# A fused attention, expert and feed-forward kernel: second unit's scores in other PSUM banks, zero products ahead of the first scores, clears moved, the last tile in halves

## The chip, the cores and the metric

The kernel runs on one core of one Trainium2 chip, as a single launch. The metric is the device time of that launch in microseconds (us). Three runs of the kernel before took 1148.23, 1147.63 and 1146.03 us; their median, 1147.63 us, is the time before.

## The reference

The reference chains three parts over 2304 tokens (4 batches of 576) of width 512. Part one is attention with 8 heads of 64: scores are scaled by 1/8, scores more than `tau` below their row's maximum are masked out, and a softmax over what is left weights the values. Part two is a mixture of 8 experts, two for each token, chosen by noisy gate logits. Part three is a feed-forward layer with a leaky rectifier whose slope is given for each hidden unit.

```python
scores = scale * np.matmul(q, k.transpose(0, 1, 3, 2))
thresh = np.max(scores, axis=-1, keepdims=True) - tau
scores = np.where(scores >= thresh, scores, -1000000000.0)
attn = np.exp(scores - np.max(scores, axis=-1, keepdims=True))
attn = attn / (np.sum(attn, axis=-1, keepdims=True) + 1e-09)
x = np.matmul(attn, v)                       # then [tokens, 512]
# experts: for each token the two largest of x@w_gate + log1p(exp(x@w_noise))*noise
out[mask] += top2_w[mask, k, None] * (np.maximum(x[mask] @ w1[e], 0.0) @ w2[e])
# feed-forward
h = x @ w_in
g = np.maximum(h, 0.0) + alpha * np.minimum(h, 0.0)
return g @ w_out
```

All inputs but `w_in` and `w_out` are 32-bit floats. The kernel splits each operand of a large product into a high and a low part (rounded to the matmul's fast 32-bit type, and the rest), and adds three products: high by high, high by low, low by high.

## The kernel before, in words

**Attention.** Work is cut into units: a unit is one batch, one pair of heads and 128 rows of queries (or the 64 rows left over, the "t" units, with both heads in one block-diagonal tile). The first 16 units are batch 0, head pair by head pair: units 0 to 3 use the operands of pair 0, units 4 to 7 those of pair 1, and so on. A unit passes these steps, each a small function:

- `s_mm` (line 386): 12 products of 288 columns on TensorE give the scores of two heads, into two tiles of two PSUM banks each (`psum_s`, two buffers, so one unit holds all four banks of this pool).
- `d1` (L401): VectorE scales the scores out of PSUM and takes the row's extreme; one instruction for each head.
- `a1` (L412): ScalarE's exponential. `thresh` (L406) makes the mask's limit.
- `d2` (L425): VectorE masks and sums, one instruction for each head.
- `t_mm` (L443, L445): nine turns of 128 by 128 on TensorE; `a2` (L455, L457) copies them out.
- `pv` (L479, L481): products with the values; then ScalarE copies the result (L497).

The loop over `i` (L818) issues, in this order, `t_mm` and `a2` of unit `i - 2`, `d1` and `a1` of unit `i`, `d2` of unit `i - 1`, `s_mm` of unit `i + 1`, and `pv` of unit `i - 3`. The order of issue is the order on every engine. `put(i, f)` files a piece of other work to be issued at iteration `i`. Among it are `split_hi` (L328, L330: ScalarE rounds a raw operand) and `do_lo` (L338: GpSimd subtracts to get the low part; ahead of it a one-element copy, L734, makes GpSimd wait for the newest row sum of `d2`). After the low part of a query operand, `tail_tile` (L322) copies 64 by 64 blocks for the "t" units. The off-diagonal blocks of those tiles are cleared once: 32 memsets at L314, ahead of everything else on GpSimd. GpSimd then clears two tiles for the values (L347), makes the last part of the first low operand (L705), runs `tail_tile(0)`, and clears a tile of zeros (L708) that iterations 9 to 23 write to DRAM.

**The first unit.** Its operands are loaded in four pieces, rounded on ScalarE (L704), and their low parts made by VectorE (three pieces, L705) and GpSimd (the fourth).

**PSUM.** Four banks belong to `psum_s`; the other four to `psum_t` (three) and `psum_v` (one), which `t_mm` and `pv` first use at iterations 2 and 3.

**Experts and feed-forward.** After attention TensorE runs the expert layers (L236, L254) and the feed-forward (L236, L1103) nearly without a break. The last step, `down_chunk` (L1087) for the last chunk, finishes four output tiles in the order 0, 2, 1, 3: 12 products of 512 columns, three for each tile, each tile followed by a copy out of PSUM (ScalarE for 0 and 2, VectorE for 1 and 3, L1096) and a store (L1098) that SyncE issues.

Of the kernel before, what the change touches and what calls it, by code (L numbers as in the profile page):

```python
# [6 lines left out]
FT = mybir.dt.float32  # L7
# [18 lines left out]
NSET = 8  # L26
SETW = 2688
DT = 2
# [7 lines left out]
def emit(tc, qt, kt, v, tau, wg, wn, noise, w1, w2, w_in, w_out, alpha, out):  # L36
# [8 lines left out]
    with (  # L45
# [57 lines left out]
        pairs = tc.tile_pool(name="psum_pairs", bufs=1, space=PSUM)  # L103
        bank_pool = [pairs.__enter__()]

        def psum_s():
            return bank_pool[0].tile([128, 2, 512], FT, name="ps_s", tag="s", bufs=2)

        def single_banks():
            pairs.__exit__(None, None, None)  # L110
            bank_pool[0] = later.enter_context(tc.tile_pool(name="psum_banks", bufs=1, space=PSUM))
# [3 lines left out]

        def psum_t(dt=FT):
            return pp.tile([128, 512], dt, name="ps_t", tag="t", bufs=3)

        def psum_v():
            return pp.tile([128, 512], FT, name="ps_v", tag="v", bufs=1)  # L120
# [190 lines left out]
        for i in range(NSET):  # L311
            for z in pair(i)[4:]:
                for h in range(2):
                    pool.memset(f32(z[h * 64:h * 64 + 64, 64 - h * 64:128 - h * 64]), 0.0)  # L314
# [76 lines left out]
        def s_bank(i):  # L391
            for h in range(nh(i)):
                st[i]["ps", h] = psum_s()
# [312 lines left out]
        tail_tile(0)  # L706
        zero = xtok_ring()
        pool.memset(zero, 0.0)  # L708
# [44 lines left out]

        for e in range(E):
            put(9 + 2 * e, zero_init, e)
# [60 lines left out]
        s_bank(0)  # L816
        s_mm(0)
        for i in range(END):  # L818
            it, iv = i - DT, i - DT - 1
            tiles, outs = 0 <= it < NU, 0 <= iv < NU  # L820
            if tiles:
                t_mm(it, 0)
                a2(it, 0)
# [263 lines left out]
        def down_chunk(j, f):  # L1087
# [6 lines left out]
            def store(t):  # L1094
                y = y_tile[0]()
                (dve.tensor_copy if last and t % 2 else act.copy)(y, acc[j][t])  # L1096
                r = (sum(sizes[:j]) + t) * 128
                sp.dma_start(out[r:r + 128], y)  # L1098

            for t in (0, 2, 1, 3) if last else range(sizes[j]):  # L1100
                ps = acc[j][t]
                for k, (x, ww) in enumerate(((0, WH), (1, WH), (0, WL))):
                    pe.matmul(ps, h[x][:, t * 128:t * 128 + 128], ww[w][:, c:c + 512],  # L1103
                              start=(f == 0 and k == 0), stop=(f == 15 and k == 2))
                if last:
                    store(t)
# [151 lines left out]
```

## Time and profile before

| | us |
|---|---|
| median of three runs | 1147.63 |
| the profiled execution, its own time | 1147.74 |
| its span, first instruction to last | 1145.9 |
| TensorE busy | 1124.0 |
| VectorE busy | 612.6 |
| ScalarE busy | 528.5 |
| GpSimd busy | 534.1 |

The profiled execution took 1147.74 us; its span is 1145.9 us, so 1.8 us lie around it. A timeline row reads: start in us from the span's start, length in us, engine, line, operation, output and inputs, sizes and count; in brackets the idle time of the engine before it and what ended that. SPq is SyncE's queue, which issues DMAs; PEld is the loading of weights. A row with a count covers several instructions that follow each other, gaps included.

### The profile page before, as it was taken

Reading aid. Unit: us, or ns where it says so; the run is one execution under the profiler, and the core shown is the slowest. Engines: PE = TensorE matmul, PEld = TensorE weight load, DVE = VectorE, ACT = ScalarE, POOL = GpSimd, SP = SyncE. Lnnn points to the kernel's source line nnn. Section 1 sums busy time; section 2 is a strip of 40 time slices with the busy share of each in tenths; the row PEclk is TensorE's granted clock in tenths of the full one; section 3 lists DMA queues with packets and bytes.
Section 4 is the critical chain, followed back from the end, with each engine's and each line's share of the span. In section 5 each row is a group of like instructions: output and inputs, shape, how many; then the busy total and the mean of one; then the engine's idle time right before and its main releaser. Section 6 shows DMA issues by size and latency. Waiting matters only on the chain.

```text
span 1145.9 us, 20653 instructions
## 1 busy us (share of the span) xinstructions
PE 1124.0 (98%) x7754; PEld 974.0 (85%) x7754; DVE 612.6 (53%) x1316; ACT 528.5 (46%) x1039; POOL 534.1 (47%) x706
## 2 busy tenths in 40 slices
PE   7999999999999999999999999999999999999997
PEld 6887888788898989888999999898888888888886
DVE  6879899699544544444444544444433443442221
ACT  7978888689344444445444545442111211121111
POOL 7556545554635455455554454484322332332221
PEclk9999999999999999999999999999999999999999
DMA  6423222232566766667767565532321321220001
GB/s 212 142 94 120 101 97 85 88 118 83 187 175 190 192 205 183 189 179 220 192 172 222 175 187 188 179 121 65 74 56 55 74 54 53 73 56 23 21 1 39
DMA packets 156553, 141.51 MB, mean 123 GB/s; under 512 B 108576, under 2 KB 109216, under 8 KB 156448
## 3 DMA queue, kind: packets, MB, share of 16 engines
q1 hardware_dynamic: 150400, 120.91, 36.1%
q0 software_dynamic: 5760, 18.88, 5.0%
q8 instruction: 63, 1.03, 0.4%
q14 instruction: 42, 0.34, 0.1%
q10 hardware_dynamic: 288, 0.34, 0.1%
HBM read 97.11 MB, written 42.99 MB: 122 GB/s over the span
## 4 chain that ended last, share of the span: by engine, by line
PE 69%; issue 3%; POOL 2%; DVE 2%; ACT 1%; DMA 1%; SPq 0%; POOLq 0%; DVEq 0%; ACTq 0%
PE ps_t L236 33%; PE ps_u L1103 17%; PE ps_u L254 16%; POOL m_pair L190 1%; PE ps_v L479 0%; DMA m_tmp<-in_w_in_dram 0%; PE ps_u L236 0%; ACT m_hh L412 0%; DMA m_v<-in_w_dram 0%; PE ps_t L216 0%; POOL m_tmp L956 0%; DVE m_tmp L401 0%; PE ps_t L443 0%; ACT m_last L455 0%; POOL m_last L190 0%
## 5 line engine op out<-in xcount | busy, mean ns | idle before, releaser
L236 PE MATMUL ps_t<-m_v,m_pair 128*128 128x384 f32 (+2 forms) x1216 | 220.1, 317 | 0.6 <-ACT m_v L220 0.3
L190 POOL TENSOR_TENSOR m_pair<-m_v,m_pair 128x512 fp32r<-128x512 f32 x108 | 143.7, 1352 | 121.8 <-ACT m_pair L184 111.3
L236 PEld LDWEIGHTS ps_t<-m_v,m_pair 128*128 128x128 f32 x1216 | 186.8, 190 | 8.8 <-ACT m_v L220 0.7
L254 PE MATMUL ps_u<-m_pair,m_hh 128*128 128x512 f32 x528 | 167.5, 390 | 0.0
L1080 DVE TENSOR_SCALAR m_tmp<-ps_t,alpha_t 128x512 f32<-128x512 f32 (+1 forms) x80 | 55.7, 697 | 208.6 <-PE ps_t L236 206.7
L247 DVE SCALAR_TENSOR_TENSOR m_gate<-ps_t,m_hh 128x384 fp32r<-128x384 f32 (+1 forms) x120 | 58.9, 493 | 169.2 <-ACT m_hh L246 169.0
L236 PE MATMUL ps_t<-m_v,m_early 128*128 128x256 f32 (+2 forms) x672 | 127.3, 320 | 0.0
L401 DVE TENSOR_SCALAR_CACHE_REDUCE m_tmp<-ps_s 128x576 f32<-128x576 f32 x144 | 106.1, 753 | 29.4 <-ACT m_last L457 12.7
L425 DVE SCALAR_TENSOR_TENSOR m_hh<-m_tmp,sm,m_hh 128x576 f32<-128x576 f32 x144 | 117.3, 847 | 0.0
L254 PEld LDWEIGHTS ps_u<-m_pair,m_hh 128*128 128x128 f32 x528 | 99.2, 188 | 20.2
L1085 POOL TENSOR_TENSOR m_v<-m_tmp,m_v 128x512 fp32r<-128x512 f32 x39 | 50.5, 1294 | 140.0 <-ACT m_v L1084 140.0
L236 PEld LDWEIGHTS ps_t<-m_v,m_early 128*128 128x128 f32 x672 | 105.8, 189 | 5.1 <-DVE m_v L224 0.4
L412 ACT ACTIVATE m_hh<-m_tmp,sm 128x576 f32<-128x576 f32 x144 | 105.5, 782 | 3.2 <-DVE m_tmp L401 3.2
L1084 ACT CAST m_v<-m_tmp 128x512 fp32r<-128x512 f32 x39 | 24.2, 621 | 173.7 <-DVE m_tmp L1081 173.7
L254 PE MATMUL ps_u<-m_pair,m_gate 128*128 128x512 f32 x264 | 103.0, 390 | 0.0
L1085 POOL TENSOR_TENSOR m_gate<-m_tmp,m_gate 128x512 fp32r<-128x512 f32 (+1 forms) x41 | 44.1, 1078 | 115.8 <-ACT m_gate L1084 109.6
L246 ACT ACTIVATE m_hh<-ps_t 128x384 fp32r<-128x384 f32 (+1 forms) x120 | 52.7, 439 | 98.5 <-PE ps_t L236 97.0
L386 PE MATMUL ps_s<-m_pair 64*128 64x288 f32 (+1 forms) x864 | 89.1, 317 | 9.0 <-ACT m_pair L704 4.4
L1103 PE MATMUL ps_u<-m_pair,m_v 128*128 128x512 f32 x396 | 95.1, 389 | 0.0
L1103 PE MATMUL ps_u<-m_pair,m_gate 128*128 128x512 f32 x360 | 88.3, 391 | 0.0
L386 PEld LDWEIGHTS ps_s<-m_pair 64*128 64x128 f32 (+1 forms) x864 | 69.4, 191 | 22.3 <-DVE m_tmp L401 11.9
L1103 PEld LDWEIGHTS ps_u<-m_pair,m_v 128*128 128x128 f32 x396 | 74.3, 188 | 15.4
(244 smaller groups left out, 1987.8 us busy)
## 6 DMA issues: line engine op xcount, KB each, us to landing
m_v<-in_w_dram SPq DMA_DIRECT2D x64, 512.0 KB, 4.0
yg<-m_tmp SPq DMA_DIRECT2D x40, 256.0 KB, 3.3
m_tmp<-in_w_in_dram SPq DMA_DIRECT2D x16, 512.0 KB, 4.3
m_tmp<-in_w_out_dram SPq DMA_DIRECT2D x16, 512.0 KB, 5.1
m_early<-in_kt_dram SPq DMA_DIRECT2D x15, 320.0 KB, 3.5
yg<-m_gate SPq DMA_DIRECT2D x18, 256.0 KB, 2.0
m_rows<-xg SPq DMA_DIRECT2D x72, 64.0 KB, 3.1
out_dram<-m_tmp SPq DMA_DIRECT2D x18, 256.0 KB, 2.4
```

The source lines that it names most:

```text
L190: eng.tensor_tensor(WL[n][:, w], raw[:, w], f32(WH[n][:, w]), op=OP.subtract)
L236: pe.matmul(ps[:, :n], w[wc[d]][:, col:col + 128], x[xx][:, d, :n], start=(k == 0), stop=(k == 11))
L246: act.activation(h, ps, AF.Relu)
L247: dve.scalar_tensor_tensor(hs[1][:, f * n:f * n + n], ps, 0.0, f32(h), op0=OP.max, op1=OP.subtract)
L254: pe.matmul(ps, a[:, o:o + 128], ww[w][:, c:c + 512], start=(f == 0 and k == 0), stop=(f == nf - 1 and k == 2))
L386: pe.matmul(u["ps", h][:, x, :288], lhs, kk[r, o:o + 288], start=(k == 0), stop=(k == 2))
L401: dve.tensor_scalar(u["sp"][:, h].rearrange("p (a b) -> p a b", a=2), ps[:, :, :288], -0.125, None, op0=OP.mult, op1=OP.min, accum_out=u[" ...
L412: act.activation(u["em"][:, h], u["sp"][:, h], AF.Exp, bias=u["sm"][:, h:h + 1], scale=-1.0)
L425: dve.scalar_tensor_tensor(u["em"][:, h], u["sp"][:, h], sm[:, 2 + h:3 + h], u["em"][:, h], op0=OP.is_le, op1=OP.mult, accum_out=acc)
L1080: dve.tensor_scalar(g, ps, 0.0, alpha_t[:, f:f + 1], op0=OP.min, op1=OP.mult)
L1085: pool.tensor_tensor(h[:, n:2 * n], g, f32(h[:, :n]), op=OP.subtract)
L1103: pe.matmul(ps, h[x][:, t * 128:t * 128 + 128], ww[w][:, c:c + 512], start=(f == 0 and k == 0), stop=(f == 15 and k == 2))
```

## The change

Four edits, all at the head or the tail of the program.

1. The scores of unit 1 go into a pool of their own, `psum_first`, in the four banks that `psum_t` and `psum_v` use later; `second_half` closes it at iteration 2 (`i == DT`) and opens `psum_second` for those two. The two pools of scores move to the other side of PSUM.
2. A tile `spare` is zeroed by VectorE, and seven products of it with itself are issued on TensorE ahead of `s_mm(0)`, into columns of the first unit's bank that the scores don't use. At iteration 2 eight turns of the identity are issued ahead of `t_mm(0)`.
3. The 32 memsets at L314 become `clear_tails`, four of them at each of the iterations 1 to 8; `tail_tile(0)` moves to iteration 5, and the memset of the tile of zeros to iteration 7.
4. In the last step, output tile 3 is computed and stored in two halves of 256 columns, the first copied by ScalarE and the second by VectorE.

```diff
-        pairs = tc.tile_pool(name="psum_pairs", bufs=1, space=PSUM)
+        pairs = tc.tile_pool(name="psum_pairs", bufs=1, space=PSUM, side="right")
...
+        half = [tc.tile_pool(name="psum_first", bufs=1, space=PSUM)]
+        half.append(half[0].__enter__())
+
+        def second_half():
+            half[0].__exit__(None, None, None)
+            half[1] = later.enter_context(tc.tile_pool(name="psum_second", bufs=1, space=PSUM))
+
         def psum_t(dt=FT):
-            return pp.tile([128, 512], dt, name="ps_t", tag="t", bufs=3)
+            return half[1].tile([128, 512], dt, name="ps_t", tag="t", bufs=3)
...
-        for i in range(NSET):
+        def clear_tails(i):
             for z in pair(i)[4:]:
                 for h in range(2):
                     pool.memset(f32(z[h * 64:h * 64 + 64, 64 - h * 64:128 - h * 64]), 0.0)
...
-                st[i]["ps", h] = psum_s()
+                st[i]["ps", h] = half[1].tile([128, 2, 512], FT, name=f"ps_f{h}") if i == 1 else psum_s()
...
-        tail_tile(0)
         zero = xtok_ring()
-        pool.memset(zero, 0.0)
...
+        for n in range(NSET):
+            put(1 + n, clear_tails, n)
+        put(5, tail_tile, 0)
+        put(7, pool.memset, zero, 0.0)
...
         s_bank(0)
+        spare = em_ring.aps[2][:, 0, :128]
+        dve.memset(spare, 0.0)
+        for _ in range(7):
+            pe.matmul(st[0]["ps", 0][:, 0, 384:], spare, spare, start=True, stop=True)
         s_mm(0)
...
+            if i == DT:
+                second_half()
+                ps = psum_v()
+                for _ in range(8):
+                    pe.transpose(ps[:, :128], ident, ident)
...
-            def store(t):
-                y = y_tile[0]()
-                (dve.tensor_copy if last and t % 2 else act.copy)(y, acc[j][t])
+            def store(t, o=0, n=512):
+                y = y_tile[0]()[:, o:o + n]
+                (dve.tensor_copy if last and (t == 1 or o) else act.copy)(y, acc[j][t][:, o:o + n])
                 r = (sum(sizes[:j]) + t) * 128
-                sp.dma_start(out[r:r + 128], y)
+                sp.dma_start(out[r:r + 128, o:o + n], y)
...
+                for o, n in ((0, 256), (256, 256)) if last and t == 3 else ((0, 512),):
+                    for k, (x, ww) in enumerate(((0, WH), (1, WH), (0, WL))):
+                        pe.matmul(ps[:, o:o + n], h[x][:, t * 128:t * 128 + 128], ww[w][:, c + o:c + o + n],
```

On TensorE the program begins, before, with the scores of units 0 to 2 (three times 12 products at L386), then the turns of unit 0 (L443, L445) and the scores of unit 3:

```order
L1254 UNCONDITIONAL_BRANCH
L386 MATMUL ps_s<-m_pair 128x288 x36
L443 MATMUL ps_t<-ident,m_hh 128x128 x8
L445 MATMUL ps_s<-ident,m_hh 128x128
L386 MATMUL ps_s<-m_pair 128x288 x12
L443 MATMUL ps_t<-ident,m_hh 128x128 x8
L445 MATMUL ps_s<-ident,m_hh 128x128
L386 MATMUL ps_s<-m_pair 128x288 x12
L479 MATMUL ps_v<-m_tmp,m_v_73 64x128 x8
L481 MATMUL ps_v<-m_tmp,m_v_73 64x128 x2
```

Each row there is a run of equal instructions; the lines from 386 to 705 stand 7 higher in the changed program. Now, with what each waits for (DVE is VectorE; `ps_f` is a tile of `psum_first`, `m_hh` holds `spare`; ten more `ps_f` rows of the same pattern and then the rest of unit 2 follow):

```order
L1274 UNCONDITIONAL_BRANCH [waits barrier_Pool_Activation_PE_DVE_SP_release]
L829 MATMUL ps_s<-m_hh 128x128 [waits DVE_49]
L829 MATMUL ps_s<-m_hh 128x128 x6
L393 MATMUL ps_s<-m_pair 128x288 [waits Activation_49]
L393 MATMUL ps_s<-m_pair 128x288 x5
L393 MATMUL ps_s<-m_pair 128x288 [waits Activation_49]
L393 MATMUL ps_s<-m_pair 128x288 x5
L393 MATMUL ps_f_186<-m_pair 128x288
L393 MATMUL ps_f_187<-m_pair 128x288
```

The seven products of the zeroed tile stand ahead of unit 0's scores and wait for VectorE; unit 1's scores wait for nothing. On VectorE, whose queue is in order, the first rows before were the three low parts (L705) and then the scores of units 0 and 1:

```order
L1254 UNCONDITIONAL_BRANCH [waits barrier_Pool_Activation_PE_DVE_SP_release]
L705 TENSOR_TENSOR m_pair<-m_early,m_pair 128x256 [waits DMAHW0_49,Activation_49]
L705 TENSOR_TENSOR m_pair<-m_early,m_pair 128x352 [waits DMAHW3_49,Activation_49]
L705 TENSOR_TENSOR m_pair<-m_early,m_pair 128x288 [waits DMAHW1_49,Activation_49]
L401 TENSOR_SCALAR m_tmp,sm_151<-ps_s 128x576 [waits PE_49] x2
```

The low parts wait for DMAs and for ScalarE. Now the memset of `spare` (L827) stands behind them:

```order
L1274 UNCONDITIONAL_BRANCH [waits barrier_Pool_Activation_PE_DVE_SP_release]
L712 TENSOR_TENSOR m_pair<-m_early,m_pair 128x256 [waits DMAHW0_49,Activation_49]
L712 TENSOR_TENSOR m_pair<-m_early,m_pair 128x352 [waits DMAHW3_49,Activation_49]
L712 TENSOR_TENSOR m_pair<-m_early,m_pair 128x288 [waits DMAHW1_49,Activation_49]
L827 MEMSET m_hh 128x128
L408 TENSOR_SCALAR m_tmp,sm_122<-ps_s 128x576 [waits PE_49] x2
```

The memset is the fourth instruction of VectorE's queue, after all three low parts of unit 0. On GpSimd, between the first operand's low part and the two low parts of head pair 1 (L338 before), the rows before were these (L734 waits for the row sums of `d2`):

```order
L314 MEMSET m_pair 64x64 x32
L347 MEMSET m_v_73 128x512
L347 MEMSET m_v_74 128x512
L705 TENSOR_TENSOR m_pair<-m_early,m_pair 128x320
L322 TENSOR_SCALAR m_pair<-m_pair 64x64 x4
L708 MEMSET m_gate 128x512
L734 COPY m_gate<-es_145 1x1
L338 TENSOR_TENSOR m_pair<-m_early,m_pair 128x288 x2
L322 TENSOR_SCALAR m_pair<-m_pair 64x64 x4
L734 COPY m_gate<-es_146 1x1
L338 TENSOR_TENSOR m_pair<-m_early,m_pair 128x320 x2
```

Behind the second pacing copy comes the low part of the key of pair 1, which unit 4 needs. Now:

```order
L354 MEMSET m_v_73 128x512
L354 MEMSET m_v_74 128x512
L712 TENSOR_TENSOR m_pair<-m_early,m_pair 128x320
L739 COPY m_gate<-es_116 1x1
L345 TENSOR_TENSOR m_pair<-m_early,m_pair 128x288 x2
L329 TENSOR_SCALAR m_pair<-m_pair 64x64 x4
L321 MEMSET m_pair 64x64 x4
L739 COPY m_gate<-es_117 1x1
L345 TENSOR_TENSOR m_pair<-m_early,m_pair 128x320 x2
L321 MEMSET m_pair 64x64 x8
```

Four of the moved clears (L321) now stand between the two low parts of pair 1, ahead of the key's.

## Rows read from the trace of the kernel before

**Rows 1.** Busy time of each engine over the whole span

```profile
PE 1124.0 (98%) x7754; PEld 974.0 (85%) x7754; DVE 612.6 (53%) x1316; ACT 528.5 (46%) x1039; POOL 534.1 (47%) x706
```

**Rows 2.** Timeline of the first 12.6 us: start, length, engine, line, operation

```profile
2.60 5.81 POOL L314 MEMSET m_pair<- 64x64 f32 x32
...
4.02 1.28 DVE L705 TENSOR_TENSOR m_pair<-m_early,m_pair 128x256 fp32r<-128x256 f32 x3 [4.02 <-ACT m_pair L704]
...
4.42 2.13 PE L386 MATMUL ps_s<-m_pair 64*128 64x288 f32 x12 [4.42 <-ACT m_pair L704]
4.98 1.22 PEld L386 LDWEIGHTS ps_s<-m_pair 64*128 64x128 f32 x10 [0.27 <-DVE m_pair L705]
6.58 0.76 DVE L401 TENSOR_SCALAR_CACHE_REDUCE m_tmp<-ps_s 128x576 f32<-128x576 f32 x1 [1.29 <-PE ps_s L386]
...
8.46 1.00 POOL L347 MEMSET m_v<- 128x512 f32 x2
...
9.69 0.76 DVE L401 TENSOR_SCALAR_CACHE_REDUCE m_tmp<-ps_s 128x576 f32<-128x576 f32 x1 [1.67 <-PE ps_s L386]
...
10.60 2.39 PE L386 MATMUL ps_s<-m_pair 64*128 64x288 f32 x12 [0.72 <-DVE m_tmp L401]
...
11.79 0.81 DVE L425 SCALAR_TENSOR_TENSOR m_hh<-m_tmp,sm,m_hh 128x576 f32<-128x576 f32 x1
...
12.03 0.52 POOL L708 MEMSET m_gate<- 128x512 f32 x1
```

**Rows 3.** Timeline from 12.6 to 20.4 us

```profile
12.68 0.18 POOL L734 COPY m_gate<-es 1x1 f32<-1x1 f32 x1
...
12.93 1.96 PE L443 MATMUL ps_t<-ident,m_hh 128*128 128x128 f32 x8
...
14.35 2.09 POOL L322 TENSOR_SCALAR m_pair<-m_pair 64x64 fp32r<-64x64 f32 x4
...
14.93 1.06 PE L386 MATMUL ps_s<-m_pair 64*128 64x288 f32 x12
...
16.50 0.17 POOL L734 COPY m_gate<-es 1x1 f32<-1x1 f32 x1
...
16.64 1.67 POOL L338 TENSOR_TENSOR m_pair<-m_early,m_pair 128x320 fp32r<-128x320 f32 x2
...
18.37 0.94 PE L386 MATMUL ps_s<-m_pair 64*128 64x288 f32 x10 [0.29 <-POOL m_pair L338]
...
19.23 1.10 PE L479 MATMUL ps_v<-m_tmp,m_v 128*64 128x128 f32 x16
```

**Rows 4.** Busy us (count) by engine in four stretches; PEclk is the granted clock

```profile
10.60:13.00 2.40, 2.39 (x13) 1.79 (x14) 2.21 (x7) 2.15 (x4) 2.08 (x6) 1.00 0.78 218
14.90:16.00 1.10, 1.10 (x14) 0.92 (x14) 0.84 (x4) 1.10 (x3) 0.97 (x3) 1.00 0.93 196
...
20.00:40.00 20.00, 20.00 (x245) 16.89 (x242) 17.27 (x47) 18.84 (x44) 10.87 (x20) 1.00 0.59 179
40.00:60.00 20.00, 19.99 (x242) 17.00 (x240) 18.05 (x49) 19.97 (x49) 13.17 (x24) 1.00 0.36 102
```

**Rows 5.** The chain of waits, feed-forward and tail: start, length, what

```profile
750.16 1.43 PE ps_t L236 x12
...
1131.31 8.17 PE ps_u L1103 x36
...
1139.51 0.69 DVE m_tmp L1096
```

**Rows 6.** SyncE's queue at the tail, and its stores' landing times

```profile
1139.55 0.33 SPq L1098 DMA_DIRECT2D out_dram<-m_tmp  x1
...
1140.23 0.33 SPq L1098 DMA_DIRECT2D out_dram<-m_tmp  x1
...
DMA to landing us min/median/max: 2.0/2.4/2.6
```

More of the change, by code (lines that the diff above doesn't have):

```diff
@@ L110, in single_banks @@
             pairs.__exit__(None, None, None)
-            bank_pool[0] = later.enter_context(tc.tile_pool(name="psum_banks", bufs=1, space=PSUM))
+            bank_pool[0] = later.enter_context(tc.tile_pool(name="psum_banks", bufs=1, space=PSUM, side="right"))
         def psum_u():
             return bank_pool[0].tile([128, 512], FT, name="ps_u", tag="u", bufs=4)
+        half = [tc.tile_pool(name="psum_first", bufs=1, space=PSUM)]
[3 more added lines that the diff above has]
+            half[1] = later.enter_context(tc.tile_pool(name="psum_second", bufs=1, space=PSUM))
         def psum_t(dt=FT):
-            return pp.tile([128, 512], dt, name="ps_t", tag="t", bufs=3)
+            return half[1].tile([128, 512], dt, name="ps_t", tag="t", bufs=3)
         def psum_v():
-            return pp.tile([128, 512], FT, name="ps_v", tag="v", bufs=1)
+            return half[1].tile([128, 512], FT, name="ps_v", tag="v", bufs=1)
         ident = cp.tile([128, 128], FT, name="ident")
@@ L1092, in down_chunk @@
             last = (j, f) == (len(sizes) - 1, 15)
-            def store(t):
-                y = y_tile[0]()
-                (dve.tensor_copy if last and t % 2 else act.copy)(y, acc[j][t])
+            def store(t, o=0, n=512):
+                y = y_tile[0]()[:, o:o + n]
+                (dve.tensor_copy if last and (t == 1 or o) else act.copy)(y, acc[j][t][:, o:o + n])
                 r = (sum(sizes[:j]) + t) * 128
-                sp.dma_start(out[r:r + 128], y)
+                sp.dma_start(out[r:r + 128, o:o + n], y)
             for t in (0, 2, 1, 3) if last else range(sizes[j]):
                 ps = acc[j][t]
[L1102 to L1106, printed above, removed]
+                for o, n in ((0, 256), (256, 256)) if last and t == 3 else ((0, 512),):
+                    for k, (x, ww) in enumerate(((0, WH), (1, WH), (0, WL))):
+                        pe.matmul(ps[:, o:o + n], h[x][:, t * 128:t * 128 + 128], ww[w][:, c + o:c + o + n],
+                                  start=(f == 0 and k == 0), stop=(f == 15 and k == 2),
+                                  skip_group_check=(j == len(sizes) - 1 and t == 3))
+                    if last:
+                        store(t, o, n)
             if f == 15 and not last:
```

## The prediction, made before the changed kernel was run

> **What bounds the kernel now.** I read the page's busy shares first, then the timeline of the head, then the stretches, and last the chain and the queue at the tail, since the change touches only the first 20 us and the last 10. TensorE is busy for 98% of the span [rows 1]: whatever time it starts its dense work later, the kernel ends later, unless a stretch has slack that takes it up. In the attention stretch there is none: from 20 to 60 us TensorE is busy 39.99 of 40 us and ScalarE 38.81 [rows 4]. So the question at the head is when TensorE gets past its last wait before 20 us. That wait is at unit 4: its scores go on at 18.37, released by GpSimd's low part of the key of pair 1 [rows 3]. GpSimd's chain to it begins with the pacing copy at 12.68, which had to wait for the second `d2` of unit 0; that ends at 11.79 + 0.81 = 12.60 [rows 2, 3]. Back from there: VectorE reads unit 0's scores from 6.58, and stands idle 1.67 us, from 8.02 to 9.69, until unit 1's scores are there, which had to wait for unit 0's banks [rows 2]. The head is thus one chain: unit 0's scores, `d1`, idle 1.67, `d1` and `d2`, pacing copy, GpSimd, unit 4.
>
> **The zero products.** They wait for a memset that is fourth in VectorE's queue, behind three low parts that run from 4.02 to 5.30 [rows 2]. The trace has no VectorE memset; it costs at least nothing and at most what one of those larger low parts takes, 1.28/3 = 0.43. I take 0.15, nearer the bottom since it reads nothing and writes half as much as the smallest. Products begin at 5.30 + 0.15 + 0.05 = 5.50, and TensorE, which would have begun scores at 4.42, can do nothing before: the scores stand behind them.
>
> What seven cost: eight 32-bit products of 128 columns with the values appear as 16 records of 1.10 us [rows 3], so such a product is two records; those run side by side on two halves of the array, and a full product fills both halves. A record of that length is one turn of 128 columns: eight in 1.96 us at 12.93 [rows 3], some 0.21 each without the drain of the last. Seven products are 14 x 0.21 = 3.0 us; if each were one record, 1.5. I take 3.0, from the row whose data type is the same. They end at 8.5.
>
> Unit 0's scores took 2.13 us, of which weights waited 0.27 for low parts [rows 2]; those are ready now, so 1.86. They end at 10.36, VectorE starts at 10.39 instead of 6.58: 3.8 us late.
>
> **Unit 1's scores in their own banks.** They follow at once, and are there before VectorE's two instructions for unit 0 (6.58 to 8.02, 1.44 us) are done. The idle 1.67 goes. `d2` of unit 0 ends 1.44 + (12.60 - 9.69) = 4.35 after VectorE's start, at 14.74 instead of 12.60: 2.14 late. The later and smaller gains on VectorE's side are worth nothing while GpSimd is later still.
>
> **The clears.** Before, GpSimd had 32 of them in 5.81 us, 0.18 each, while nothing waited for it [rows 2]; removing them from there gains nothing. Now four stand between the low parts of pair 1: 4 x 0.18 = 0.73 us. A clear could be stretched by VectorE as the copies of `tail_tile` are (four in 2.09 us, 0.52 each [rows 3]): then 2.1. I take 0.73, because a memset that ran beneath `d2`, at 12.03, took 0.52 for 512 columns, and two of that size without it took 1.00 [rows 2]. The other moved pieces stand behind the key's low part: `tail_tile(0)` ten iterations before its first reader, the tile of zeros two before SyncE's first store of it. They cost nothing, and if that cover went, their own 2 us on GpSimd.
>
> GpSimd's chain: pacing copy at 14.74 + 0.08 = 14.82; 16.50 - 12.68 = 3.82 to the second pacing copy, and 0.73 for clears; 16.64 + 1.67 - 16.50 = 1.81 to the end of the low part: 21.18. Unit 4 goes on at 21.24 instead of 18.37, 2.87 late. Behind it on TensorE wait `pv` of unit 0 and every later turn, and for these ScalarE, which has no room to catch up [rows 4].
>
> **The eight turns of the identity** need banks that unit 1's second `d1` frees at 10.39 + 4 x 0.72 = 13.27, and take 1 to 2 us (eight for 1.96 at the slow pace). `t_mm` of unit 0 can begin some 14.0 by its own input, the first of the two `d2` that end at 14.74, so it may be a microsecond late. That is hidden: between it and 21.24 TensorE has only two units' turns and one unit's scores to do, under 6 us even at the slow pace. Without that cover it would cost that microsecond.
>
> **TensorE's clock.** [...] I take 0.4.
>
> [...]
>
> **The carry.** 2.87 - 0.4 = 2.47 us late at unit 4. Nothing further back runs on a clock of its own: loads and weights are issued as buffers come free, so they shift along, and what follows is TensorE's dense chain.
>
> **The tail.** TensorE's last 36 products end at 1139.48; VectorE's copy takes 0.69 from 1139.51; SyncE issues the last store at 1140.23, the one before at 1139.55 [rows 5, 6]. Now three products of 512 columns (0.227 each, 36 in 8.17) become six of 256 (12 in 1.43, 0.119 each): 0.68 becomes 0.72. The last copy, of half the columns, takes 0.35 at least (half of 0.69), about 0.42, and ends at 1139.97. But there are two stores where one was, and each holds SyncE for 0.33 and some 0.06 between: after the one at 1139.55 they go at 1139.94 and 1140.33. The last goes 0.1 later than before; the faster copy buys nothing. It carries half the bytes; landing took 2.0 to 2.6, so half a tile can save from nothing to 0.6; I take 0.35. Net -0.25, from -0.5 to +0.1.
>
> **The sum.** 1147.74 (the profiled execution, 0.11 above the median of the runs shown) + 2.47 - 0.25 = 1149.96; set against the median, 1149.85. From the bounds: 1.4 us late (memset at nothing, early clock, tail at its best) to 3.3 (slow clock, memset 0.43, tail at its worst). About 0.2%, 2.3 us, is what a measurement of this kernel can tell from no change, and 2.2 lies just below it. I forecast 1149.8: later by a fifth of a percent, a hair inside that bound.
>
> **The rivals.**
> - *Clears stretched.* If the four clears, or the copies ahead of them, fall beneath more of unit 1's `d2` than before, each takes 0.52 and not 0.18: 1.36 more, and the key's low part is at 22.5. For it: four copies of `tail_tile` took 2.09. Against: the memset at 12.03. Time 1147.74 + 2.47 + 1.36 - 0.25 = 1151.3, slower; it decides once clears add over 0.1, since the sum lies that near the bound.
> - *Cheap products.* One record each, 1.5 us, or a clock that rises within them: unit 0's scores end at 8.9, everything is 1.5 sooner: 1147.74 + 2.87 - 1.5 - 0.25 = 1148.9, no change. Against it stands the 16 for 8 of [rows 3].
> [...]
>
> **How the numbers follow.** Forecast 0.73, with its own range 1149.1 to 1151.0 by the bounds, and from 1148.2 with the spread of the three runs before: 0.42 of the chance within the 0.2%, 0.31 beyond. Clears stretched 0.13 (0.01 within, 0.12 slower). Cheap products 0.09 (0.07 within, 0.01 each side). As it says 0.05 (0.03 faster, 0.02 within). Faster 0.04, within 0.2% 0.52, slower 0.44. The range for 8 in 10, 1147.6 to 1151.3, takes in the cheap products with that spread and the stretched clears up to the price taken; it leaves out the last rival.
>
> **What would show it.** Right: no TensorE record before about 5.4; 14 records of products in some 3 us; VectorE's first `d1` at 9.6 to 10.4 and no idle time before unit 1's; four clears between 18 and 20; unit 4 released by GpSimd between 20.4 and 21.4; then the same rows as before, shifted by the same 2 to 3 us as far as 1130; SyncE's last store 0.1 later against the last product. Wrong: products at 1 to 4 us, unit 4 released by VectorE or not waiting, or a shift that shrinks between 20 and 300 us: then there was slack in the attention stretch that I take to be full.

## The result, and the profile after

The changed kernel takes 1154.8 us (median of six runs, 1152.04 to 1156.23), the kernel before 1147.65: a ratio of 1.006, 95% interval 1.0047 to 1.0073. It is slower, by 7 us where 2.2 were forecast, and lies outside the range. The profiled execution took 1156.23 us with a span of 1154.5; it is the longest of the six. One of the six executions of the kernel before was slow, at 1847.64 us, and the ratio takes fast ones alone.

Busy shares of the page, which answer to [rows 1]:

```profile
PE 1129.1 (98%) x7779; PEld 978.3 (85%) x7779; DVE 614.6 (53%) x1317; ACT 529.0 (46%) x1040; POOL 535.1 (46%) x706
```

TensorE is 5.1 us busier, of which the products and turns that the change adds are some 4.4; the rest, and the rest of the time, is idling and half pace. Where this happens, the timeline of the head shows (start, length, engine, line, operation; it answers to [rows 2, 3]):

```profile
5.23 0.17 DVE L827 MEMSET m_hh<- 128x128 f32 x1
...
5.45 3.36 PE L829 MATMUL ps_s<-m_hh 128*128 128x128 f32 x14 [5.45 <-DVE m_hh L827]
...
10.35 1.22 PE L393 MATMUL ps_f<-m_pair 64*128 64x288 f32 x12
...
10.58 0.76 DVE L408 TENSOR_SCALAR_CACHE_REDUCE m_tmp<-ps_s 128x576 f32<-128x576 f32 x1 [5.19 <-PE ps_s L393]
...
14.04 0.81 DVE L432 SCALAR_TENSOR_TENSOR m_hh<-m_tmp,sm,m_hh 128x576 f32<-128x576 f32 x1
...
14.93 0.18 POOL L739 COPY m_gate<-es 1x1 f32<-1x1 f32 x1 [8.88 <-DVE m_hh L432]
...
16.60 2.09 POOL L329 TENSOR_SCALAR m_pair<-m_pair 64x64 fp32r<-64x64 f32 x4
...
18.73 0.69 POOL L321 MEMSET m_pair<- 64x64 f32 x4
...
19.48 0.64 POOL L739 COPY m_gate<-es 1x1 f32<-1x1 f32 x1
...
20.01 2.36 DVE L432 SCALAR_TENSOR_TENSOR m_hh<-m_tmp,sm,m_hh 128x576 f32<-128x576 f32 x1
...
20.08 1.66 POOL L345 TENSOR_TENSOR m_pair<-m_early,m_pair 128x320 fp32r<-128x320 f32 x2
...
21.80 1.57 PE L393 MATMUL ps_s<-m_pair 64*128 64x288 f32 x10 [2.00 <-POOL m_pair L345]
```

The reader is to see three things. The head up to `d2` of unit 0 is as forecast: products at 5.45 in 14 records, `d1` at 10.58, `d2` ending at 14.85, 2.2 late. GpSimd's chain behind it is longer than in [rows 3] by the clears (0.69) and by the second pacing copy (0.64, there 0.17). And TensorE, which waited 0.29 us for unit 4 before, waits 2.00, and its ten scores then take 1.57 instead of 0.94.

The windows of after say why (us, busy us and count of PE, PEld, DVE, ACT, POOL, then the granted clock, DMA share, GB/s), beside [rows 4]. The line that stands alone behind them is the window 24 to 28 us of the kernel before:

```profile
20.00:24.00 4.00, 2.20 (x18) 1.93 (x20) 2.97 (x5) 1.13 (x4) 2.85 (x11) 0.65 0.25 72
24.00:28.00 4.00, 4.00 (x27) 3.34 (x27) 2.32 (x8) 2.00 (x5) 1.44 (x3) 0.50 0.00 2
28.00:40.00 12.00, 12.00 (x155) 10.31 (x155) 9.58 (x26) 11.11 (x27) 7.25 (x26) 1.00 0.12 31
40.00:60.00 20.00, 19.65 (x234) 16.11 (x229) 18.19 (x45) 19.05 (x47) 14.68 (x33) 1.00 0.56 184
```

```profile
24.00:28.00 4.00, 4.00 (x48) 3.50 (x48) 3.34 (x9) 3.75 (x11) 3.75 (x8) 1.00 0.51 147
```

In the wait for unit 4 the granted clock falls from 1.00 to 0.50 at 21.2 us, and it stays there until 28.0. From 24 to 28 us TensorE runs 27 records where the kernel before ran 48 at clock 1.00. That is what the forecast did not have.

Not every execution seems to pay this. The mean granted clock was 0.997 in the two shortest executions of the changed kernel (1152.04 and 1152.82 us) and 0.992 to 0.994 in the four others (1154.54 to 1156.23). The 0.003 between the profiled one (0.994) and the shortest is some 3.4 us of TensorE's time, which is what 6.8 us at half clock take away (an estimate from these means; of the other executions no trace was kept).

To place the 7 us, I took the same VectorE instruction in both traces; how much later it starts (us) at eight places, named by their time in the kernel before. The rows below it are those of the experiments that follow. Each row is one profiled execution, and some lie far from the median of their kernel: after 1.4 us above it, e5 4.6 above, e9 1.5 above, e12 and e17 1.1 below.

```
place in before       13.5   24.1   37.7   58.1   95.0  204.8  242.7 1132.2
after                 1.97   5.48   6.19   7.06   6.92   7.44   8.57   8.22
e3_turns_in_wait      1.33   2.80   2.80   3.46   3.33   3.08   3.69   4.09
e5_clears_back        1.94   4.83   5.55   5.55   5.54   5.86   8.91   9.14
e9_banks_late_clears -1.97   0.36   0.37   1.54   1.32   1.74   2.92   3.20
e11_banks_only       -0.67   1.15   1.17   1.19   1.18   1.81   3.03   3.13
e12_tails_behind     -1.98  -2.32  -2.31  -2.31  -2.32  -1.85  -3.19  -3.00
e14_after_tails      1.71   1.35   1.36   1.37   1.36   1.07   4.68   4.28
e15_late_products     1.37   1.11   1.13   1.15   1.14   0.94   4.59   4.93
e16_early_products   -2.03  -2.39  -2.39  -2.39  -2.38  -2.40   1.72   1.61
e17_two_products     -1.93  -2.28  -2.26  -2.24  -2.26  -2.62  -2.91  -2.70
```

So in after: 2.0 at the start; 3.43 at unit 4 (21.80 against 18.37); 6.2 once the half clock is over; 0.75 more at 40 to 48 us; about 1.1 more at 205 to 243 us; then nothing up to the tail, whose 0.4 comes last:

```profile
1146.30 3.02 SPq L1116 DMA_DIRECT2D out_dram<-m_tmp  x5
...
1147.39 0.37 ACT L1114 COPY m_tmp<-ps_u 128x256 f32<-128x256 f32 x1 [0.44 <-PE ps_u L1122]
...
1147.82 0.62 PE L1122 MATMUL ps_u<-m_last,m_gate 128*128 128x256 f32 x3 [0.46 <-ACT m_tmp L1114]
1148.53 0.43 DVE L1114 COPY m_tmp<-ps_u 128x256 f32<-128x256 f32 x1 [0.79 <-PEq L1206]
```

Beside [rows 5, 6]: the second half's three products, which were to follow at once, wait 0.46 us for ScalarE's copy of the first half, which reads the same tile.

### The profile page after: what moved, and what is told of

The parts are those of the page before. It is cut to its first block, busy times and chain, and to the rows that moved or that the text cites. A ratio compares the mean times of both kernels' runs of the same rounds, so it can differ in the third digit from the quotient of the medians.

```text
span 1154.5 us, 20706 instructions
## 1 busy us (share of the span) xinstructions
PE 1129.1 (98%) x7779; PEld 978.3 (85%) x7779; DVE 614.6 (53%) x1317; ACT 529.0 (46%) x1040; POOL 535.1 (46%) x706
## 5 line engine op out<-in xcount | busy, mean ns | idle before, releaser
L432 DVE SCALAR_TENSOR_TENSOR m_hh<-m_tmp,sm,m_hh 128x576 f32<-128x576 f32 x144 | 120.7, 870 | 0.0
L393 PE MATMUL ps_s<-m_pair 64*128 64x288 f32 (+1 forms) x852 | 85.8, 314 | 5.4 <-DVE m_tmp L408 2.9
L450 PE MATMUL ps_t<-ident,m_hh 128*128 128x128 f32 x576 | 81.3, 280 | 6.2 <-DVE m_hh L432 3.8
```

Source lines behind the costliest of these rows:

```text
L393: pe.matmul(u["ps", h][:, x, :288], lhs, kk[r, o:o + 288], start=(k == 0), stop=(k == 2))
L432: dve.scalar_tensor_tensor(u["em"][:, h], u["sp"][:, h], sm[:, 2 + h:3 + h], u["em"][:, h], op0=OP.is_le, op1=OP.mult, accum_out=acc)
L450: pe.transpose(ps[:, j * 128:j * 128 + 128], emf[:, o + j * 128:o + j * 128 + 128], ident)
```

## The experiments

The kernel before was timed again beside each group of runs. Its medians were 1147.89 us for e1 to e4, 1149.05 for e5, e6, e9 and e11, 1148.00 for e7, e12 and e13, 1147.82 for e14, 1148.92 for e15 and e16, 1149.09 for e17 and e18. Each ratio is against its own; times of different groups can differ by over 1 us for this alone.

**Which part costs.** The changed kernel without its products:

```diff
-        spare = em_ring.aps[2][:, 0, :128]
-        dve.memset(spare, 0.0)
-        for _ in range(7):
-            pe.matmul(st[0]["ps", 0][:, 0, 384:], spare, spare, start=True, stop=True)
```

> The changed kernel without the seven products of the zeroed tile and without its memset; all else as changed. Theory A (the late products delay unit 0's scores by 3.8 us, that makes the wait at unit 4 long, and the long wait lets TensorE's clock fall): scores start at 4.4 again, VectorE's idle 1.67 us ahead of unit 1 is gone, unit 4 goes on at 17.4 to 18.4 us, no half-clock stretch near 20 us, time 1147 to 1148.5 (the tail still costs 0.4). Theory B (the moved clears and the longer GpSimd chain do the damage whatever the products): unit 4 still goes on 1 us or more later than 18.37, a wait of about 2 us on TensorE stays, time 1150 or more.

Measured 1149.35 us, ratio 1.0012 (1.0003 to 1.0021): the late products are worth 5.4 of the 7. VectorE was 2 us ahead of before at 13.5, yet the wait for unit 4 was 2.00 us again and the clock fell behind it, at 18.4: the lead was gone at 24 us. Neither theory fits whole: unit 4 went on at 17.84, as A said, but the wait and the fall stayed.

The same products, with the memset ahead of the low parts:

```diff
+        spare = em_ring.aps[2][:, 0, :128]
+        dve.memset(spare, 0.0)
         for i, (_, raw, hi, lo, c0, c1) in enumerate(first):
```

> The changed kernel with the memset of the zeroed tile ahead of VectorE's three low parts, so that the products wait for nothing that is late. Theory A: products from about 1 to 4 us, scores at 4.4, perhaps already at the full pace, unit 4 at 16.5 to 18 us, time 1146 to 1148. Theory B: as without products, 1150 or more. If products are worth nothing when early, the time is that of the kernel without them, within 1 us.

Measured 1149.63, ratio 1.0022 (1.0012 to 1.0032). They ran at 1.13 to 4.4 us and held nothing back; unit 4 went on at 17.84, as without them. Early products gain nothing at the start.

**The clock in the wait.** The changed kernel with turns of the identity put into the wait:

```diff
+            if i == 3:
+                for _ in range(18):
+                    pe.transpose(st[4]["ps", 0][:, 0, 384:], ident, ident)
             if i + 1 < NU:
                 s_mm(i + 1)
```

> The changed kernel with 18 more turns of the identity (some 2 us) on TensorE just ahead of unit 4's scores, where it stands idle for 2.00 us; nothing else is different, and GpSimd's low part that ends the wait comes when it came. Theory A (the clock falls because of that wait, and the half clock costs 2.8 us after it): no half-clock stretch between 20 and 30 us, unit 4 still at 21.5 to 22, time 2 to 3.5 us below the changed kernel, 1151.5 to 1152.8. Rival (the growth of the delay from 3.4 to 6.2 us after unit 4 comes from GpSimd and VectorE, whose instructions block each other there): 1154 to 1156, as changed.

Measured 1152.03, ratio 1.004 (1.0026 to 1.0053), 2.8 us below after. Timeline line and windows of this kernel:

```profile
18.75 2.18 PE L865 MATMUL ps_s<-ident 128*128 128x128 f32 x18 [0.35 <-DVE m_tmp L408]
```

```profile
20.00:24.00 4.00, 4.00 (x48) 3.39 (x47) 3.61 (x7) 1.07 (x5) 2.23 (x10) 1.00 0.27 74
24.00:28.00 4.00, 4.00 (x48) 3.33 (x48) 2.89 (x9) 4.00 (x10) 2.69 (x7) 1.00 0.05 6
```

The turns compute nothing that is used. With them the clock stays 1.00, 48 records run from 24 to 28 us as in the kernel before, and the shift stays 2.80 from 24.1 to 37.7 us, where after's grew from 3.43 at unit 4 to 6.19: the fall costs 2.8 us. (The two rows differ by 3.39 at 37.7 us, but 0.64 of that stood there at 13.5: in e3 unit 0's scores took 1.14 us and not 1.81.)

The kernel e2 shows the price without an edit: its five executions at a mean clock of 0.997 or 0.998 have a median of 1148.85 us, the six at 0.992 to 0.995 one of 1152.16. In after, the two groups named above lie 3.2 us apart by their medians.

**The clears.** At their old place:

```diff
-        for n in range(NSET):
-            put(1 + n, clear_tails, n)
-        put(5, tail_tile, 0)
-        put(7, pool.memset, zero, 0.0)
+        for i in range(NSET):
+            clear_tails(i)
...
```

> The changed kernel with all clears, tail_tile(0) and the tile of zeros back at their old place, ahead of the values' tiles; products, banks, turns and tail as changed. Theory A (products delay the head by 2.1 us at unit 0's masks; clears add their own time to GpSimd's chain): GpSimd's key part 0.7 to 1.2 us sooner than in the changed kernel, unit 4 at 20.4 to 21.1, its wait 0.8 to 1.3 us and not 2.0; the extra 0.75 us between 40 and 48 us gone. If the clock falls all the same, time 1152.5 to 1153.5; if the wait is now too short for that, 1149.5 to 1151. Theory B (the products alone explain the 7 us): 1154 to 1155.

Measured 1152.48, ratio 1.003 (1.0018 to 1.0042). The wait was 1.34 us, and the shift is flat from 37.7 to 95 us: the 0.75 at 40 to 48 us belonged to the clears and the zero tile ahead of a later key's low part. In the profiled execution the clock still fell, from 20.6 to 27.4 us; but that one took 1157.10, and the five others, at a mean clock of 0.997 or 0.998, took 1151.80 to 1153.09. So the median is that of a kernel whose clock seems to have held: 3.4 us above the kernel before beside it, where the changed kernel's two executions at 0.997 stand 4.4 and 5.2 above theirs.

Two iterations later:

```diff
-            put(1 + n, clear_tails, n)
+            put(3 + n, clear_tails, n)
```

> The changed kernel with the clears two iterations later (from 3 to 10 instead of 1 to 8), so that none stands ahead of the key's low part of pair 1. Theory A: unit 4 0.7 to 1.2 us sooner, as with the clears back, since only the four between query and key counted there; a delay of some 0.7 us stays somewhere later, where other clears stand ahead of a low part: 1150.5 to 1153.5. If the place of the clears doesn't matter: 1154 to 1155.

Measured 1154.65, ratio 1.0051 (1.0039 to 1.0063), which overlaps the interval of after: no gain that can be told. The wait fell to 1.34, but the later clears stood ahead of later low parts and cost 1.2 at 40 to 58 us.

**The tail alone**, on the kernel before:

```diff
-            def store(t):
+            def store(t, o=0, n=512):
...
+                for o, n in ((0, 256), (256, 256)) if last and t == 3 else ((0, 512),):
```

> The kernel before with the tail's edit alone (the last tile in halves). By the record of the changed kernel, in which the second half's products waited 0.46 us for the copy of the first half: 0.3 to 0.5 us above the kernel before. By the prediction's term: 0.25 below it. Within noise of no change by either; the trace's last products, copies and stores tell.

Measured 1148.71, ratio 1.0003 (0.9994 to 1.0013): no difference that can be told, and the 0.46 us wait stood there as in after. The tile computed whole and copied by two engines:

```diff
+                (act if last and t == 3 and not o else sp).dma_start(out[r:r + 128, o:o + n], y)
...
+                    for o, n in ((0, 256), (256, 256)) if t == 3 else ((0, 512),):
+                        store(t, o, n)
```

> The kernel before, with the last tile computed whole as before but copied in two halves, by ScalarE and VectorE at once, each with its own store. Theory (the halves of the change lost time because the second half's products stood behind the first half's copy, 0.46 us): with no such wait the last copy shrinks from 0.69 to about 0.4 us, 1147.5 to 1147.8, ratio 0.9996 to 0.9999. Rival (two stores at the end cost as much as the shorter copy gains, or the two copies of one tile take turns): 1147.9 to 1148.5.

Measured 1148.27, ratio 1.0004 (0.9994 to 1.0013). Timeline of its end:

```profile
1137.77 0.37 ACT L1096 COPY m_tmp<-ps_u 128x256 f32<-128x256 f32 x1 [0.77 <-PE ps_u L1103]
...
1138.41 0.42 DVE L1096 COPY m_tmp<-ps_u 128x256 f32<-128x256 f32 x1 [0.63 <-DMA out_dram<-m_tmp]
```

The time is the rival's, but its reason isn't shown. The second copy began 0.27 us after the first had ended, and by its row it waited for a DMA: the copies of the last step write to a ring of four tiles and now need five, so the fifth waited for the first store of the step, issued at 1136.34 and landed at 1138.32. Whether two copies of one tile would take turns, this run can't tell. As written here, halving the last tile buys nothing in either form.

**The banks alone**, with the clears from iteration 3 and with the clears where they were:

```diff
-                st[i]["ps", h] = psum_s()
+                st[i]["ps", h] = half[1].tile([128, 2, 512], FT, name=f"ps_f{h}") if i == 1 else psum_s()
...
+            if i == DT:
+                second_half()
```

> Of the change only unit 1's own banks and the clears, from iteration 3; no products, no turns, the old tail. Theory A: VectorE has unit 1's scores 1.7 us sooner, GpSimd's chain begins 1.7 us sooner, unit 4 at 16.7 to 17.2; a wait of 1.2 us or more stays there, since all ahead of it came sooner too. The gain of 1.2 to 1.7 us is kept if the clock holds: 1146 to 1147; if it falls: 1147.5 to 1149.

Measured 1149.27, ratio 1.0003 (0.9994 to 1.0011): a lead of 2 us at 13.5, lost at unit 4 (wait 1.19).

> The kernel before with unit 1's own banks alone. GpSimd's first 32 clears now end at 8.4 and its chain begins with the first row sums at about 11.0, so tail_tile(0) and the tile of zeros, which ran from 10.2 to 12.6 before, stand in its way: unit 4 at 17.8 to 18.4, nearly as before, and TensorE waits 1.5 to 2 us there. Theory A: time 1147 to 1148 if the clock holds, 1149 to 1151 if it falls in that wait. If banks are simply worth the idle time that they remove: 1146.

Measured 1150.53, ratio 1.0017 (1.0008 to 1.0026). GpSimd's clears and first low part were late for the faster VectorE: TensorE waited 2.33 us for that low part at 10.96, and the clock fell there. Unit 4 went on at 19.52, later than expected.

**Where the lead goes.** If the wait for GpSimd at unit 4 eats it, GpSimd's order is to be changed. What stands between the two low parts of pair 1 is `tail_tile`, 2.09 us [rows 3], whose first reader is unit 16:

```diff
-                if part == "q":
+                if part == "q" and n > 3:
                     tail_tile(n)
...
+        for n in range(6):
+            clear_tails(n)
         zero = xtok_ring()
...
+        for i, n in ((3, 1), (3, 0), (6, 2), (9, 3)):
+            put(i, tail_tile, n)
+        for i, n in ((3, 6), (6, 7)):
+            put(i, clear_tails, n)
```

> The banks alone (no zero products, no turns ahead, old last tile), with two moves on GpSimd: the four tail blocks of pairs 0 to 3, which no unit reads before unit 16, are made in iterations 3, 6 and 9 and no longer between a query's and a key's low part, and six of the eight clears stand behind GpSimd's first low part, where it idles 6.2 to 11.0 us in the kernel with the banks and late clears alone. Theory (unit 4's wait for GpSimd's key low part is what eats the banks' lead and lets TensorE's clock fall): the key low part of pair 1 ends some 2 us sooner, unit 4's scores start at about 15.5 us (there 17.2, before 18.4), the wait of 1.2 goes, the granted clock stays 1.0 from its rise on, VectorE's landmarks stand 1.5 to 2.5 us before those of before at 24 to 38 us, and the time is about 1146 us, ratio 0.998 to 0.999. Rival (the lead would be lost at the next wait in any case: the loads or the next pairs' low parts hold the units behind): unit 4 is early, the landmarks at 40 us are back within 0.5 us of before, and the time is 1147.5 to 1148.5.

Measured 1145.61, ratio 0.9977 (0.9968 to 0.9986): faster than both kernels. Its timeline:

```profile
6.00 4.35 POOL L321 MEMSET m_pair<- 64x64 f32 x24
...
9.35 0.81 DVE L432 SCALAR_TENSOR_TENSOR m_hh<-m_tmp,sm,m_hh 128x576 f32<-128x576 f32 x1
...
10.98 0.18 POOL L741 COPY m_gate<-es 1x1 f32<-1x1 f32 x1 [0.63 <-DVE m_hh L432]
...
14.31 1.68 POOL L345 TENSOR_TENSOR m_pair<-m_early,m_pair 128x320 fp32r<-128x320 f32 x2
...
16.04 0.94 PE L393 MATMUL ps_s<-m_pair 64*128 64x288 f32 x10 [0.19 <-POOL m_pair L345]
```

Unit 4 waits 0.19 us, its scores take 0.94, the clock does not fall, and the lead of 2.3 us stands from 24 to 95 us. It grows to 3.2 at 243 us: in this trace the clock also holds behind the wait near 218 us, where that of the kernel before is at 0.50 from 219.6 to 223.0.

> The kernel before, with the tail blocks of pairs 1 to 3 made in iterations 3, 6 and 9 instead of between the query's and the key's low part; no banks, nothing else. Theory: in the kernel before unit 4's scores wait 0.29 us for GpSimd and VectorE's chain is as late as GpSimd's, so there is next to nothing to gain: 1147.5 to 1148.0, ratio 0.9995 to 1.0003. Rival (GpSimd's order alone sets the start of unit 4, banks or not): unit 4 starts 1 us or more sooner, 1146.5 to 1147.

With only the first and third of those edits on the kernel before (pairs 1 to 3): 1147.79, ratio 1.0001 (0.9992 to 1.001). This part of GpSimd's order (the clears stayed where they were) is worth nothing until the banks have made VectorE and TensorE earlier.

The same order in the whole changed kernel:

> The changed kernel whole (late zero products, turns, tail in halves) with GpSimd's order of e12_tails_behind: tail blocks of pairs 0 to 3 in iterations 3, 6 and 9, six clears behind its first low part. Theory (the shift that was predicted is right, and what the prediction lacked is the wait at unit 4 with the clock's fall behind it): the products still run at 5.5 to 8.4 us and VectorE stands about 2.0 us behind the kernel before at 10 to 17 us, but unit 4 waits under 0.7 us, the granted clock does not fall before 200 us, the shift stays at 2.0 to 2.5 us up to 95 us, and with 0.4 for the tail the time is 1150.0 to 1150.8, ratio about 1.002. Rival (the products themselves or the dense start bring the fall, whatever GpSimd does): the clock goes to 0.5 between 18 and 30 us and the time is 1152.5 or more.

Measured 1152.22, ratio 1.0038 (1.0024 to 1.0052). Up to 200 us the theory held: no fall, a shift of 1.4 that shrinks to 1.07 (less than expected; unit 0's scores took 1.46 us, in after 1.81). Then 3.6 us came at 205 to 243 us, and the expected time was missed by 1.4.

**The 3 us at 205 to 243.** There GpSimd sends rows by an indirect scatter and waits for it. To e12 the products alone were added, first late (memset as in the change), then early:

> e12_tails_behind (banks, GpSimd's order) with the seven zero products and their memset as the change has them, behind VectorE's three low parts; no turns, old last tile. Theory (the products cost only what they hold back at the start): VectorE stands 1.1 to 1.4 us behind the kernel before at 20 to 95 us, GpSimd's wait for the scatter near 215 us is 1.57 as in the kernel before, and the time is 1149.0 to 1149.6. Rival (with the products the dispatch near 220 us waits longer as well, as in the six profiles of kernels with products, 2.0 to 3.15 against 1.57 in the eight without): the wait is 2.0 or more, TensorE idles 2.8 us or more behind it, and the time is 1150.3 to 1151.5.

Measured 1152.42, ratio 1.0036 (1.0022 to 1.0049): the rival, and more (wait 3.13). Its trace also has a fall of the clock that GpSimd's order did not prevent, from 15.8 to 19.2 us, behind a wait of 1.12 us for `d2` of unit 0 (the turns that filled this place in e14 are not in this kernel):

```profile
15.00:20.00 5.00, 4.65 (x32) 3.90 (x34) 4.99 (x13) 4.33 (x10) 3.50 (x6) 0.66 0.84 262
```

This fall cost nothing that can be seen: unit 4's scores go on at 19.36 without a wait, and the shift is 1.37 ahead of it and 1.11 behind it. (In e14, without that fall, TensorE waited there for GpSimd's low part, 0.19 us, so half pace seems to have used up idle time.)

> e12_tails_behind with the same seven products, but their memset ahead of VectorE's low parts, so that they run at 1.1 to 4.1 us while the first loads land. Theory (products cost only what they hold back): the landmarks stand 2.2 to 2.4 us ahead of the kernel before at 20 to 95 us as without products, the scatter's wait is 1.57, and the time is that of e12, 1145.0 to 1146.2. Rival (the presence of the products lengthens the dispatch): the same lead up to 200 us, a wait of 2.0 or more near 213 us, 1147.0 to 1148.5.

Measured 1148.69, ratio 0.9999 (0.999 to 1.0008): the rival again, 0.2 us above its range. Against the kernel before beside each, e12 gains 2.4 us and e16 0.2, so these products cost some 2.2, though the lead is 2.40 at 204.8. Timelines of e12, then of e16:

```profile
211.29 1.25 POOL L674 DMA_INDIRECT xg<-m_gate,posi  x1 [0.16 <-POOL m_gate L673]
...
214.33 0.18 POOL L438 COPY es<-sm 64x1 f32<-64x1 f32 x1 [1.57 <-DMA xg<-m_gate,posi]
...
218.08 0.23 ACT L613 ACTIVATE m_gate<-m_gate 128x24 f32<-128x24 f32 x1 [2.68 <-POOL m_gate L606]
```

```profile
211.28 1.07 POOL L674 DMA_INDIRECT xg<-m_gate,posi  x1 [0.16 <-POOL m_gate L673]
...
215.87 0.18 POOL L438 COPY es<-sm 64x1 f32<-64x1 f32 x1 [3.29 <-DMA xg<-m_gate,posi]
...
219.65 1.09 PE L450 MATMUL ps_t<-ident,m_hh 128*128 128x128 f32 x4 [4.62 <-DVE m_hh L432]
```

The scatter is issued at the same time and lands 1.5 us later. More hangs on it: behind it TensorE idles 4.62 us, in e12 2.27, and in e16 the clock is at 0.50 from 219.0 to 225.8 us, in e12 not at all. The DMA view of e16 from 212.9 to 215.4 us, and of e12 from 213.1 to 213.9, the stretches of the scatter's packets (busy tenths of the 16 engines in 40 slices; queue, packets, MB, share):

```profile
DMA  9969497996200000000000040000020000141000
...
q0 software_dynamic: 80, 0.26, 26.7%
q8 instruction: 1, 0.02, 2.5%
```

```profile
DMA  4949949099099944994999499994990510000000
...
q0 software_dynamic: 80, 0.26, 80.3%
```

In e16 a 16 KB packet of the instruction queue lies among the scatter's 80; four of its rows come 0.7 us or more after the others. In e12 that packet starts 1.1 us behind the scatter's end. From the DMA records of all traces (first and last moment of the scatter's 64 row packets, start of the 16 KB packet, GpSimd's wait):

```
                    scatter's rows   fetch    wait
before              214.97-215.74   216.88    1.57
e12_tails_behind    213.12-213.88   214.99    1.57
e17_two_products    212.36-213.13   214.28    1.57
after               222.76-224.13   222.19    2.24
e14_after_tails     216.05-218.32   215.98    3.15
e16_early_products  212.93-215.34   213.37    3.29
e18_small_products  215.98-217.62   215.60    2.51
```

In the eight kernels without products up to here the packet starts behind the scatter's end (by 0.07 to 1.2 us), and the rows take 0.77; in the eight with all seven it overlaps the scatter, and they take 1.19 to 2.41. So the packet's place goes with the delay in all these traces; that it causes the delay is argued from this. Two runs were to move the packet by the number of instructions alone:

```diff
-        for _ in range(7):
+        for _ in range(2):
```

> e16_early_products_alone with two zero products instead of seven. Theory (what costs is where a 16 KB fetch of instructions falls: in the traces it starts 0.44 us after the scatter's first packet in e16 and 1.87 after it in e12, at 24 TensorE instructions a us, and the scatter's packets take 0.76; 28 instructions ahead move it by 1.4): 8 instructions move it by 0.4, to about 1.5 us, still behind the scatter; GpSimd's wait is 1.57 again and the time is that of e12, 1145.2 to 1146.2. Rival (products as such lengthen the dispatch, in proportion): a wait of about 2.0, 1146.4 to 1147.2.

Measured 1145.97, ratio 0.9973 (0.9964 to 0.9983): the packet behind the scatter, the wait 1.57 and the time as expected, the rival out. But the packet had not moved: it starts 1.92 us after the scatter's first packet, in e12 1.87, where 1.5 was expected. So the run fits the theory and does not show what sets the packet's place.

```diff
-        for _ in range(7):
-            pe.matmul(st[0]["ps", 0][:, 0, 384:], spare, spare, start=True, stop=True)
+        for _ in range(16):
+            pe.matmul(st[0]["ps", 0][:, 0, 384:416], spare, spare[:, :32], start=True, stop=True)
```

> e16_early_products_alone with sixteen products of 32 columns in place of the seven of 128: 64 TensorE instructions ahead instead of 28. Theory (place of the fetch): 64 instructions move it by about 3.3 us, to 1.4 before the scatter's first packet, so that it ends about where the scatter begins; the wait near 213 us is 1.57 to 1.9 and the time 1145.5 to 1147.0, more instructions but faster than e16's 1148.7 (unit 0's scores may start up to 0.8 us late). Rival (the more added instructions, the longer the dispatch): a wait of 3 us or more, 1148.5 or more.

Measured 1151.11, ratio 1.0021 (1.0011 to 1.003): a miss. The small products were not short:

```profile
1.13 7.04 PE L832 MATMUL ps_s<-m_hh 128*128 128x32 f32 x32 [1.13 <-DVE m_hh L711]
```

At 0.22 us a record, nearly as long as with 128 columns (14 in 3.36, 0.24), they held unit 0 back to 8.1 us; the packet still touched the scatter. This run tells only that twice the instructions did not make the scatter worse than in e16 (1.64 us against 2.41).

## Why the prediction was wrong

- *Products, unit 0, `d2`.* Right. Start 5.45 (5.50), 14 records ending at 8.81, 0.07 behind the start of unit 0's scores at 8.74; `d1` 10.58 (10.39); no idle before unit 1's; `d2` ending at 14.85 (14.74). No product ran before 5.45 and each made two records, so "cheap products" and "as it says" are out.
- *The clears.* Four at 0.69 us (0.73), not stretched. But "they cost nothing", said of the other moved pieces, was wrong: clears and the zero tile ahead of later low parts cost 0.75 at 40 to 48 us, as e5 shows.
- *GpSimd's chain.* 21.80 for 21.24. What was missing is the second pacing copy, 0.64 instead of 0.17, beside VectorE's `d2`.
- *The 0.4 for the clock.* It was the author's estimate, and no run shows such a term. What the runs showed is a time of unit 0's scores that differs from kernel to kernel, with the same products ahead of them: 1.81 us in this execution (1.86 less 0.4 was taken), where the clock's first record, 1.00, is at 10.9, behind them; 1.46 in e14; 1.14 in e3 and e15, where the head was 0.6 earlier. It is not what failed.
- *The carry.* This step failed. "Nothing further back runs on a clock of its own" overlooked TensorE's. The working had both ends of the wait at unit 4, and even called it cover for the turns: TensorE's work ahead of it, denser and at full pace, and GpSimd's later low part. The wait between them, 0.29 before, became 2.00, in it the granted clock fell, and TensorE's work up to 28 us ran at half pace: 2.8 us (27 records from 24 to 28 us, before 48), returned when e3 filled the wait and absent when e12's and e14's order removed it. It also overlooked the dispatch: in after, with 44 more TensorE instructions ahead of it (28 of the products, 16 of the turns), a 16 KB packet of the instruction queue lies on the scatter, GpSimd's wait became 2.24 us (1.57) and TensorE's behind it 3.58 (2.29), and these longer waits make the 1.1 us; that the packet causes them is argued, not shown. The half clock behind that wait lasts as long in both kernels (229.4 to 232.8 us, before 219.6 to 223.0).
- *The tail.* −0.25 became about +0.4: the price of three more products was right, the wait of 0.46 for the copy of the first half was not seen.

Sum by the trace of after: 3.4 at unit 4 (2.47 taken), 2.8 for the clock (0), 0.75 for clears (0), 1.1 at the dispatch (0), 0.4 at the tail (−0.25), 8.45, with a span 8.6 longer; medians differ by 7.1, since this execution is the slowest of the six. Of what the forecast lacked, the clock is the largest term but not the only one: the two executions at a mean clock of 0.997 are 4.4 and 5.2 us above the kernel before, and they too lie outside the forecast's range.

What stays open: a further idle 1.1 us of TensorE near 235 to 248 us in the profiles of e5, e6, e9, e11 and e14 to e18 and in none of the others. What decides in which executions the clock falls was not found, nor what sets the place of the packet. Why four of the scatter's rows come late by more than the packet's own 1 us was not tried either.

## What to carry to other kernels

When a change makes one engine's work denser ahead of a wait, work out both ends of that wait: here the granted clock fell at some of TensorE's waits of 1.12 to 2.00 us, and one fall cost more than its wait, 2.8 us at a wait of 2.00. A lead won on one engine is kept only if the chain that feeds the next meeting point is shortened with it; here the banks were worth nothing alone, GpSimd's order nothing alone, and both together 0.23%. Work that seems free because it runs in an idle stretch still has a place in a queue (the moved clears and the zero tile cost 0.75 us at 40 to 48 us) and in the instruction stream (in the kernels with all seven products the scatter's rows took 1.19 to 2.41 us, without products 0.77).

## What the runs showed of the hardware

VectorE's `d2` took 2.36 us at 20.01 instead of 0.81, while GpSimd's low part ran from 20.08 to 21.74; in e12_tails_behind the `d2` at 9.35, beside GpSimd's clears (6.00 to 10.35), took 0.81. In the kernel before, the `d2` at 17.54 took 1.39, beside the second half of a low part on GpSimd (17.46 to 18.31). What in these GpSimd instructions makes the difference no run shows.

The clock fell in or just behind waits of 1.12 us (e15), 1.19 (e9), 1.34 (e5, e6) and 2.00 us (e1, e2, after), and not in e3, whose wait was filled with turns. Waits of the same length did not always bring it: at the place of e15's 1.12 us, e16 and e17 waited 1.13 and 1.14 and kept 1.00. Near 220 us TensorE waited 2.3 us in nine profiles; five lost the clock there (before, e4, e9, e11, e13) and four kept it (e1, e7, e12, e17). The nine others waited 2.81 to 4.62 us there, and all lost it. So at waits of 1.12 to 2.3 us the fall came in some profiles and not in others.

The fetch of the table above is a packet of the instruction queue, q8: 16 KB, about 1 us (1.00 in before, 0.96 in after, 1.37 in e14). In the nine profiles where it overlapped the scatter on which GpSimd waits, the scatter's rows took 1.19 to 2.41 us, in the nine others 0.76 or 0.77.
